# Third and fourth tile of an expert as one pair of 256 tokens, and PSUM banks of their own for first layers inside branches

## The chip, the cores and the metric

The kernel runs on one core of one Trainium2 chip. The metric is the device time of one execution in microseconds, the median of the runs shown. The engines are TensorE (PE: matmuls, PEld: weight loads), VectorE (DVE), ScalarE (ACT), GpSimd (POOL) and SyncE (SP, transfers only).

## The reference

Three parts in a row: attention with 32 global and 512 local positions, a dense block of width 2048 with a squared relu, and a block of eight experts. The change lies in the last. Cut to what matters:

```
do_compute = x @ w_skip > 0            # x: 2176 tokens of 512
logits = x[do_compute] @ w_gate        # eight experts
e_idx, gate_w = argmax and its softmax weight
for e in range(8):                     # w1[e]: 512 x 1024, w2[e]: 1024 x 512
    h = maximum(x[mask_e] @ w1[e], 0)
    y[mask_e] = gate_w * (h @ w2[e])
out[do_compute] = x[do_compute] + y
```

How many tokens an expert has is known only when the kernel runs.

## The kernel before

Tokens are first sorted into slots of 128 for each expert. An expert's tokens are worked in tiles of 128. A **tile** (`expert_tile`) is a generator in nine steps: `first` makes the hidden layer of 1024 as two blocks of 512 columns, each 4 x 3 matmuls with 128 tokens as the stationary operand and a block of 512 weight columns streaming past. Every product is done in three matmuls, high x high, high x low and low x high, as each operand is kept as a rounded high part and a remainder (names ending in `h` and `l`, or the two halves of `xp`). `turn` transposes the relu's result (four transposes, `ertr`), because the second layer needs it with the hidden index on the partitions, and splits it on ScalarE and VectorE (`split`). `second` is 24 matmuls of 512 columns into `y`. A VectorE step (`eo`) scales by the gate weight and adds the token itself, and GpSimd scatters the rows to `out`.

Before a tile runs, GpSimd **gathers** its tokens from DRAM (`gather`, into `xg`), and `prepare` transposes them (four transposes, `etr`) and splits them into `xp`. Tile 0 of every expert always runs; while it runs, the weights of the next expert are fetched, rounded on ScalarE (`e42h` is the high part of fetch 42; eight fetches an expert, so e24 to e31 are expert 3's and e32 to e39 expert 4's), and the low parts are made on VectorE (`e42l`). Each later tile stands inside the arm of a branch on the expert's number of tokens (`more`, `tc.If`): the arm of tile j starts the gather of tile j + 1, runs tile j with the preparation of tile j + 1 after its sixth step, and ends with the branch for tile j + 1. After the fifth tile there is a loop. `hint` tells the engines ahead of time which way the next branch will go. The order of instructions is the order of the code; nothing is rescheduled. Each engine passes the branch by itself, and waits behind it are on counts that each engine's semaphore has reached, the arm's share included.

The hidden layer's results lie in two PSUM banks with the tag `h`, in tile 0 and in every arm alike. `s` and `o` are the tags of two banks that attention and routing use before the experts begin, and `x2` has two banks for `y`.

The dense block (`ffn_block`) already does its first layer the other way round: weights stationary, 256 tokens moving, so that the hidden index comes out on the partitions and nothing is transposed.

## Time and profile before

| | us |
|---|---|
| median of three runs | 740.95 (740.13 to 741.21) |
| the profiled execution | 740.43 |
| its span, first to last instruction | 738.6 |
| PE busy in it | 708.3 |
| DVE, ACT, POOL busy in it | 420.2, 393.3, 168.5 |
| expert 1, first matmul of tile 0 | 595.12 |
| expert 3: tile 0, 1, 2, 3, first matmul each | 622.14, 635.26, 647.58, 660.02 |
| expert 4, 5, 6, 7, first matmul of tile 0 | 673.06, 686.51, 700.07, 713.64 |

A profile's times belong to one execution. Busy is the time in which an engine had an instruction in work; PE's ends are modelled, so two PE rows overlap on paper, and the step from start to start is the real pace. PE fetches its own code: the queue called q8 instruction carries pieces of 16 KB.

### The profile page before, as it was taken

What the parts mean: (1) busy time and instruction counts of PE and PEld (TensorE: products, weight loads), DVE (VectorE), ACT (ScalarE), POOL (GpSimd) and SP (SyncE); (2) the same over time, 40 slices, a digit from 0 to 9 for tenths busy, and PEclk for the clock granted to TensorE, in tenths of its full rate; (3) what the DMA queues carried; (4) which work ended last, traced back from release to release, by engine and by line L of the source; (5) the groups of instructions that cost most, each with busy time, mean ns of one, the idle gap of its engine ahead of it and who ended that gap; (6) DMA issues with size and microseconds to landing.
All of it is one profiled execution on the core that took longest, in us unless ns stands there. A gap on an engine that the chain in (4) does not pass through costs nothing. (4 is left out here: it accounts for less than half of the span.)

```text
span 738.6 us, 18687 instructions
## 1 busy us (share of the span) xinstructions
PE 708.3 (96%) x7509; PEld 588.1 (80%) x7509; DVE 420.2 (57%) x1077; ACT 393.3 (53%) x968; POOL 168.5 (23%) x213
## 2 busy tenths in 40 slices
PE   6689999999999999999999999999999999999996
PEld 4466677889888888888888988888878777887774
DVE  1889955853652463556165265342576279615993
ACT  5767567665544553534555454343354368515781
POOL 5000144461121121212112111122132222222121
PEclk8799999999999999999999999999999999999999
DMA  9999461073146114063501204100475779615920
GB/s 269 249 296 302 173 152 36 19 182 47 35 107 145 48 37 105 2 133 77 123 31 37 70 14 143 59 28 3 163 210 171 270 239 339 241 46 180 337 71 17
DMA packets 119462, 96.07 MB, mean 130 GB/s; under 512 B 84997, under 2 KB 92165, under 8 KB 119348
## 3 DMA queue, kind: packets, MB, share of 16 engines
q1 hardware_dynamic: 108304, 71.01, 35.0%
q10 hardware_dynamic: 8292, 15.48, 6.4%
q0 software_dynamic: 2752, 8.07, 3.4%
q8 instruction: 71, 1.16, 0.7%
q14 instruction: 43, 0.35, 0.2%
HBM read 82.28 MB, written 13.18 MB: 129 GB/s over the span
## 5 line engine op out<-in xcount | busy, mean ns | idle before, releaser
L180 POOL TENSOR_TENSOR gl<-g,gh 128x256 fp32r<-128x256 f32 x107 | 79.7, 745 | 302.2 <-ACT gh L179 154.7
L696 PE MATMUL h<-xh,w_in 128*128 128x256 f32 x464 | 134.7, 290 | 0.7 <-ACT xh L179 0.7
L697 PE MATMUL h<-xl,w_in 128*128 128x256 f32 x464 | 129.5, 279 | 0.3 <-DVE xl L180 0.3
L698 PE MATMUL h<-xh,w_in 128*128 128x256 f32 x464 | 129.7, 279 | 0.0
L721 PE MATMUL acc<-w_out,gh 128*128 128x512 f32 x232 | 97.7, 421 | 1.5 <-ACT gh L179 1.5
L723 PE MATMUL acc<-w_out,gl 128*128 128x512 f32 x232 | 91.9, 396 | 0.2
L722 PE MATMUL acc<-w_out,gh 128*128 128x512 f32 x232 | 91.6, 395 | 0.0
L696 PEld LDWEIGHTS h<-xh,w_in 128*128 128x128 f32 x464 | 87.0, 188 | 4.2 <-ACT xh L179 0.9
L700 ACT ACTIVATE g<-h 128x256 f32<-128x256 f32 x128 | 48.8, 382 | 76.7 <-PE h L698 43.3
L697 PEld LDWEIGHTS h<-xl,w_in 128*128 128x128 f32 x464 | 87.3, 188 | 2.7 <-DVE xl L180 0.5
L698 PEld LDWEIGHTS h<-xh,w_in 128*128 128x128 f32 x464 | 87.0, 188 | 0.0
L429 ACT ACTIVATE sm<-sm,mx 128x128 f32<-128x128 f32 x120 | 46.7, 391 | 49.5 <-DVE mx L427 49.5
L737 DVE TENSOR_TENSOR g<-h,g 128x256 f32<-128x256 f32 x53 | 22.2, 420 | 85.4 <-ACT g L700 85.3
L179 ACT CAST gh<-g 128x256 fp32r<-128x256 f32 x116 | 47.2, 407 | 42.2 <-DVE g L737 40.2
L723 PEld LDWEIGHTS acc<-w_out,gl 128*128 128x128 f32 x232 | 43.6, 188 | 12.0 <-POOL gl L180 1.4
L721 PEld LDWEIGHTS acc<-w_out,gh 128*128 128x128 f32 x232 | 43.6, 188 | 8.5 <-ACT gh L179 1.9
L722 PEld LDWEIGHTS acc<-w_out,gh 128*128 128x128 f32 x232 | 43.8, 189 | 5.6
L180 DVE TENSOR_TENSOR ehl<-ertr,ehl 128x512 fp32r<-128x512 f32 x26 | 18.0, 691 | 38.8 <-ACT ehl L179 38.8
L863 POOL DMA_INDIRECT xg<-x2d,slots x19 | 23.6, 1243 | 47.6 <-DVE ehl L180 15.0
L422 DVE TENSOR_TENSOR sm<-sc,mask 128x512 f32<-128x512 f32 x30 | 20.6, 687 | 23.8 <-PE sc L409 23.1
L894 ACT ACTIVATE er<-eh 128x512 f32<-128x512 f32 x26 | 15.6, 600 | 34.6 <-PE eh L891 31.1
L251 POOL TENSOR_TENSOR w_in<-st_raw_in,w_in 128x512 fp32r<-128x512 f32 x10 | 13.0, 1307 | 81.2 <-ACT w_in L247 81.2
(724 smaller groups left out, 1584.0 us busy)
## 6 DMA issues: line engine op xcount, KB each, us to landing
st_e<-in_moe_w_dram SPq DMA_DIRECT2D x52, 512.0 KB, 6.0
vr<-in_v_l_dram SPq DMA_DIRECT2D x49, 192.0 KB, 4.0
st_raw_in<-in_moe_w_in_dram SPq DMA_DIRECT2D x16, 512.0 KB, 7.4
st_raw_out<-in_moe_w_out_dram SPq DMA_DIRECT2D x16, 512.0 KB, 5.6
st_e<-in_moe_w_dram ACTq DMA_DIRECT2D x12, 512.0 KB, 4.8
x2d<-x ACTq DMA_DIRECT2D x19, 256.5 KB, 4.4
st_gv<-in_v_l_dram SPq DMA_DIRECT2D x8, 512.0 KB, 4.1
out_dram<-x ACTq DMA_DIRECT2D x16, 256.0 KB, 4.1
```

Of the source, the lines that this page charges most:

```text
L179: nc.scalar.copy(hi, src)
L180: (lo_engine or nc.vector).tensor_tensor(out=lo, in0=src, in1=hi.bitcast(F32), op=ALU.subtract)
L429: nc.scalar.activation(sm[:, hh, :], sm[:, hh, :], AF.Exp, bias=mx[:, hh:hh + 1], scale=SCALE, accum_out=osum[:, 2 * hh + g:2 * hh + g + 1],)
L696: nc.tensor.matmul(h, lhsT=wh, rhs=xh[:, k, :], start=(k == 0), stop=False)
L697: nc.tensor.matmul(h, lhsT=wh, rhs=xl[:, k, :], start=False, stop=False)
L698: nc.tensor.matmul(h, lhsT=wl, rhs=xh[:, k, :], start=False, stop=(k == KD - 1))
L700: nc.scalar.activation(g, h, AF.Relu)
L721: nc.tensor.matmul(acc[z], lhsT=gh[:, c], rhs=wh, start=first_one, stop=False)
L722: nc.tensor.matmul(acc[z], lhsT=gh[:, c], rhs=wl, start=False, stop=False)
L723: nc.tensor.matmul(acc[z], lhsT=gl[:, c], rhs=wh, start=False, stop=last_one)
L737: nc.vector.tensor_tensor(out=square, in0=h, in1=g, op=ALU.mult)
L863: nc.gpsimd.indirect_dma_start(out=gathered(e, j), out_offset=None, in_=x2d, in_offset=bass.IndirectOffsetOnAxis(ap=gi, axis=0), bounds_ch ...
```

## The change

For every expert but the first, the third and fourth tile are done together when the expert has over 384 tokens; with 257 to 384 tokens the third tile is done alone, in the other arm of that branch. The arm of tile 1 now gathers and prepares both. `expert_pair` does the first layer as the dense block does, with the two tiles' 256 tokens moving, one unit of 128 hidden positions after the other, and the second layer of a unit after the first layer of the next. The hidden units go to two banks in turn, `s` and `o`, each with its relu on ScalarE and its low part on VectorE. The fifth tile is gathered and prepared inside its own arm. The branch behind the pair gets no hint. And `inner` gives every first layer inside an arm the banks `s` and `o`, so that `h` is tile 0's alone (of expert 0, tile 0's and tile 1's, which both stand outside of branches).

```diff
     def gathered(e, j):
-        return xgs[(0, e % 3) if j == 0 else (1, e % 2) if j % 2 else (2, 0)]
+        if j == 3 and e:
+            return xgs[0, e % 3]
+        return xgs[(0, e % 3) if j == 0 else (1, e % 2) if j % 2 or (j == 4 and e) else (2, 0)]
...
     def prepared(e, j):
-        return xps[(0, e % 2) if j == 0 else (1, 0) if j == 1 else (2, j % 2)]
+        if j > 1:
+            return [x[:, :, j % 2 * P:(j % 2 + 1) * P] for x in joint()]
+        x = xps[(0, e % 2) if j == 0 else (1, 0)]
+        return x[:, 0], x[:, 1]
...
+    def inner(in_arm, z, name):
+        tag = ("s", "o")[z % 2] if in_arm else "h"
+        return ps.tile([P, 512], F32, tag=tag, bufs=BANKS[tag], name=name)
...
-                hs[fb] = ps.tile([P, 512], F32, tag="h", bufs=2, name=f"eh_{name}_{fb}")
+                hs[fb] = inner(j > (not e), fb, f"eh_{name}_{fb}")
...
+    def expert_pair(e, sis):
+
+        ph, pl = joint()
+        ys, gs = [], {}
+
+        def first(f):
+            fb, c = divmod(f * P, DM)
+            cols = slice(c, c + P)
+            h = inner(True, f, f"eph_{e}_{f}")[:, 0:BLK]
+            for k in range(KD):
+                wh, wl = ew[e, 1, (fb, k)]
+                nc.tensor.matmul(h, lhsT=wh[:, cols], rhs=ph[:, k, :], start=(k == 0), stop=False)
+                nc.tensor.matmul(h, lhsT=wh[:, cols], rhs=pl[:, k, :], start=False, stop=False)
+                nc.tensor.matmul(h, lhsT=wl[:, cols], rhs=ph[:, k, :], start=False, stop=(k == KD - 1))
+            gh, gl = gs[f] = [sb(n, 3, [P, BLK], f"e{n}_{e}_{f}", F32R) for n in ("gh", "gl")]
+            nc.scalar.activation(gh, h, AF.Relu)
+            nc.vector.scalar_tensor_tensor(
+                out=gl, in0=h, scalar=0.0, in1=gh.bitcast(F32), op0=ALU.max, op1=ALU.subtract
+            )
+
+        def second(f):
+            gh, gl = gs.pop(f)
+            wh, wl = ew[e, 2, f]
...
+            for z in range(2):
+                c = slice(z * P, (z + 1) * P)
+                nc.tensor.matmul(ys[z], lhsT=gh[:, c], rhs=wh, start=(f == 0), stop=False)
+                nc.tensor.matmul(ys[z], lhsT=gh[:, c], rhs=wl, start=False, stop=False)
+                nc.tensor.matmul(ys[z], lhsT=gl[:, c], rhs=wh, start=False, stop=(f == KE - 1))
+
+        first(0)
+        for f in range(KE):
+            if f + 1 < KE:
+                first(f + 1)
+            second(f)
...
         def least(e, j):
+            if e and j == 2:
+                return 3 * P
...
-                if j + 1 < UNROLL:
-                    hint(e, j + 1)
-                    gather(e, j + 1, slot(gidx, e, j + 1))
+                if e and j == 4:
+                    gather(e, j, slot(gidx, e, j))
+                    prepare(e, j)
+                    following = ()
+                else:
+                    following = (2, 3) if e else range(j + 1, UNROLL)[:1]
+                    if following:
+                        hint(e, j + 1)
+                for z in following:
+                    gather(e, z, slot(gidx, e, z))
                 for u, _ in enumerate(expert_tile(e, j, slot(sidx, e, j))):
-                    if u == 5 and j + 1 < UNROLL:
-                        prepare(e, j + 1)
-                more(e, j + 1)
+                    if 5 <= u < 5 + len(following):
+                        prepare(e, following[u - 5])
+                more(e, j + 1) if j != 1 else more_two(e)
...
+        def more_two(e):
+
+            with tc.If(n_tok[e] > least(e, 2), label=f"more{e}_2") as branch:
+                expert_pair(e, [slot(sidx, e, z) for z in (2, 3)])
+                more(e, 4)
+            with branch.Else():
+                with tc.If(n_tok[e] > 2 * P):
+                    for _ in expert_tile(e, 2, slot(sidx, e, 2)):
+                        pass
```

On PE, the start of expert 3's third tile. Ahead of it stand the last matmuls of tile 1 (`y_3_1`) and the branch. Before, a tile follows:

```order
L905 MATMUL y_3_1_10354<-e31l_10283,ehl_3_1_10353 128x512
L906 MATMUL y_3_1_10354<-e31h_10259,ehl_3_1_10353 128x512
L1166 COMPARE_AND_BRANCH
L1151 REGISTER_ALU
L1225 BRANCH_PREFETCH_HINT
L889 MATMUL eh_3_2_0_10456<-e24h_9623,xp2_0_8023 128x512 [waits Activation_49]
L890 MATMUL eh_3_2_0_10456<-e24l_9644,xp2_0_8023 128x512
L891 MATMUL eh_3_2_0_10456<-e24h_9623,xp2_0_8023 128x512 [waits DVE_49]
```

Now the pair follows (`eph_3_0` is its first unit):

```order
L916 MATMUL y_3_1_10539<-e31l_10465,ehl_3_1_10538 128x512
L917 MATMUL y_3_1_10539<-e31h_10441,ehl_3_1_10538 128x512
L1249 COMPARE_AND_BRANCH
L958 MATMUL eph_3_0_10628<-xp2_0_8023,e24h_9714 128x256 [waits Activation_49]
L959 MATMUL eph_3_0_10628<-xp2_1_8024,e24h_9714 128x256 [waits DVE_49]
L960 MATMUL eph_3_0_10628<-xp2_0_8023,e24l_9735 128x256
```

Tokens and weights have changed places, the columns are 256, the hint is gone, and the wait for VectorE's low part of the tokens moved from the third matmul to the second.

Further on in the same place on PE, where the hidden layer goes over into the second layer. Before, in tile 2 (`ertr` are the transposes of the hidden layer):

```order
L891 MATMUL eh_3_2_1_10471<-e27h_10202,xp2_0_8023 128x512
L904 MATMUL y_3_2_10455<-e28h_10208,ehl_3_2_10454 128x512 [waits Activation_49]
L905 MATMUL y_3_2_10455<-e28l_10224,ehl_3_2_10454 128x512
L906 MATMUL y_3_2_10455<-e28h_10208,ehl_3_2_10454 128x512 [waits DVE_49]
L904 MATMUL y_3_2_10455<-e28h_10208,ehl_3_2_10454 128x512
L905 MATMUL y_3_2_10455<-e28l_10224,ehl_3_2_10454 128x512
L906 MATMUL y_3_2_10455<-e28h_10208,ehl_3_2_10454 128x512
L276 MATMUL ertr_3_2_1_10499<-ident_70,er_3_2_1_10491 128x128 [waits Activation_49]
```

Now, in the pair (`yp_3_0` and `yp_3_1` are the outputs of the two halves, `egh` and `egl` the parts of a hidden unit):

```order
L960 MATMUL eph_3_1_10645<-xp2_0_8023,e25l_9754 128x256
L974 MATMUL yp_3_0_10662<-e28h_10390,egh_3_0_10641 128x512 [waits Activation_49]
L975 MATMUL yp_3_0_10662<-e28l_10406,egh_3_0_10641 128x512
L976 MATMUL yp_3_0_10662<-e28h_10390,egl_3_0_10642 128x512 [waits DVE_49]
L974 MATMUL yp_3_1_10663<-e28h_10390,egh_3_0_10641 128x512
L975 MATMUL yp_3_1_10663<-e28l_10406,egh_3_0_10641 128x512
L976 MATMUL yp_3_1_10663<-e28h_10390,egl_3_0_10642 128x512
L958 MATMUL eph_3_2_10670<-xp2_0_8023,e24h_9714 128x256
```

The transposes are gone, and the second layer of a unit waits for ScalarE once and for VectorE once, with the next unit's first layer ahead of it.

On PE, the end of expert 3's arms, ahead of expert 4's first tile (`eh_4_0_0`). Before, the ends of four arms:

```order
L1166 UNCONDITIONAL_BRANCH [waits PE_49] x4
L889 MATMUL eh_4_0_0_10836<-e32h_10281,xp0_0_8020 128x512 [waits Activation_49]
L890 MATMUL eh_4_0_0_10836<-e32l_10302,xp0_0_8020 128x512 [waits DVE_49]
L891 MATMUL eh_4_0_0_10836<-e32h_10281,xp0_0_8020 128x512 [waits DVE_49]
L889 MATMUL eh_4_0_0_10836<-e32h_10281,xp0_0_8020 128x512
```

Now the other arm's tile 2 (`y_3_2`) stands there, and three ends behind it:

```order
L917 MATMUL y_3_2_11033<-e31h_10441,ehl_3_2_11032 128x512
L1253 UNCONDITIONAL_BRANCH
L1253 UNCONDITIONAL_BRANCH [waits PE_49]
L1227 UNCONDITIONAL_BRANCH [waits PE_49]
L900 MATMUL eh_4_0_0_11109<-e32h_10463,xp0_0_8020 128x512 [waits Activation_49]
L901 MATMUL eh_4_0_0_11109<-e32l_10484,xp0_0_8020 128x512 [waits DVE_49]
```

From the branch behind the pair to expert 4's first matmul lie the arm of the fifth tile, the loop and now the other arm as well.

## Rows read from the trace of the kernel before

**Rows 1.** The page's first table: busy us (share of the span) x instructions.

```profile
PE 708.3 (96%) x7509; PEld 588.1 (80%) x7509; DVE 420.2 (57%) x1077; ACT 393.3 (53%) x968; POOL 168.5 (23%) x213
```

**Rows 2.** Busy us by stage: tile 2, tile 3, expert 5 (columns in the first line).

```profile
core 0: us, PE busy (x) PEld busy (x) DVE busy (x) ACT busy (x) POOL busy (x), PEclk, DMA share, GB/s
...
647.58:660.02 12.44, 12.44 (x62) 10.19 (x61) 2.83 (x4) 2.96 (x5) 2.06 (x2) 1.00 0.13 42
660.02:673.06 13.04, 12.60 (x61) 10.01 (x60) 3.23 (x5) 4.32 (x7) 2.05 (x2) 1.00 0.14 43
...
686.51:700.07 13.56, 13.29 (x64) 10.43 (x65) 12.58 (x14) 11.11 (x14) 3.07 (x3) 1.00 0.97 337
```

**Rows 3.** Timeline (start, us, engine, line, what, [idle before]): two ends of tiles.

```profile
647.36 0.39 PE L906 MATMUL y<-e31h,ehl 128*128 128x512 f32 x1
...
647.58 0.40 PE L889 MATMUL eh<-e24h,xp 128*128 128x512 f32 x1
...
672.23 0.39 PE L906 MATMUL y<-e31h,ehl 128*128 128x512 f32 x1
...
673.06 0.50 PE L889 MATMUL eh<-e32h,xp 128*128 128x512 f32 x1 [0.44 <-PEq L1166]
```

**Rows 4.** Instructions of tile eh in expert 3: xcount, duration ns min/median/max, first and last start.

```profile
L889 PE MATMUL eh<-e24h,xp x8: 389/393/498, 622.1 to 660.7; 128*128 128x512 f32 x8
```

**Rows 5.** Timeline of PE: one group of transposes inside the second layer.

```profile
644.39 0.60 PE L276 MATMUL etr<-ident,xg 128*128 128x128 f32 x4
...
644.75 0.48 PE L904 MATMUL y<-e30h,ehl 128*128 128x512 f32 x1
...
645.06 0.39 PE L905 MATMUL y<-e30l,ehl 128*128 128x512 f32 x1
```

**Rows 6.** Timeline of PE in the dense block; group of its weight loads (busy, mean ns).

```profile
519.93 0.28 PE L696 MATMUL h<-xh,w_in 128*128 128x256 f32 x1
...
521.35 0.40 PE L721 MATMUL acc<-w_out,gh 128*128 128x512 f32 x1
...
522.75 0.39 PE L721 MATMUL acc<-w_out,gh 128*128 128x512 f32 x1
...
L697 PEld LDWEIGHTS h<-xl,w_in 128*128 128x128 f32 x464 | 87.3, 188 | 2.7 <-DVE xl L180 0.5
```

**Rows 7.** Timeline there: a unit's last matmul, its relu, VectorE's step.

```profile
521.23 0.28 PE L698 MATMUL h<-xh,w_in 128*128 128x256 f32 x1
...
521.61 0.39 ACT L700 ACTIVATE g<-h 128x256 f32<-128x256 f32 x1 [1.18 <-PE h L698]
...
522.03 0.42 DVE L737 TENSOR_TENSOR g<-h,g 128x256 f32<-128x256 f32 x1 [1.07 <-ACT g L700]
```

**Rows 8.** Timeline: a prepared tile's low part, and the start of expert 3's tile 1.

```profile
634.69 0.69 DVE L180 TENSOR_TENSOR xp<-etr,xp 128x512 fp32r<-128x512 f32 x1
...
635.03 0.39 PE L906 MATMUL y<-e31h,ehl 128*128 128x512 f32 x1
...
635.26 0.39 PE L889 MATMUL eh<-e24h,xp 128*128 128x512 f32 x1
```

**Rows 9.** The gather in tile 1: timeline, and DMA issues (us to landing).

```profile
638.79 1.02 POOL L863 DMA_INDIRECT xg<-x2d,slots  x1 [0.31 <-issue]
...
xg<-x2d,slots POOLq DMA_INDIRECT x1, 3.5
```

**Rows 10.** Timeline: from expert 4 to expert 5.

```profile
685.84 0.40 PE L906 MATMUL y<-e39h,ehl 128*128 128x512 f32 x1
...
686.51 0.50 PE L889 MATMUL eh<-e40h,xp 128*128 128x512 f32 x1 [0.27 <-ACTq L1166]
...
688.38 1.23 DVE L834 TENSOR_TENSOR e42l<-st_e,e42h 128x1024 fp32r<-128x1024 f32 x1 [0.40 <-DVEq L1166]
...
689.66 0.19 PEld L890 LDWEIGHTS eh<-e42l,xp 128*128 128x128 f32 x1 [0.30 <-DVE e42l L834]
```

**Rows 11.** Fetches of PE's code (packets, MB, share): whole span, and from 670 to 671.

```profile
q8 instruction: 71, 1.16, 0.7%
...
q8 instruction: 1, 0.02, 5.5%
```

## The prediction

> **What bounds the kernel now.** I read the page's busy table first: TensorE is busy 96% of the span [rows 1]. Then the table by stages, cut at the starts of the tiles of expert 3 and after [rows 2]: in the two tiles that the change fuses, VectorE and ScalarE have 2.8 to 4.3 us of work in 12 to 13 us, TensorE has 12.4 to 12.6 at a granted clock of 1.00. There, and only there, TensorE alone sets the pace. In the experts that follow, VectorE is busy 12.58 of 13.56 us, so those stages have two limits. Last the timeline of TensorE: tile 2 begins 0.22 us after the last matmul of tile 1 was issued, which is the ordinary step, so a branch that is taken costs nothing; from the last matmul of tile 3 to the first of expert 4 it is 0.83 us, so the branch that is not taken, with the ends of the arms behind it, costs 0.60 [rows 3]. Whatever is saved on TensorE between 647.58 and 673.06 should arrive at the end in full: the transfers are quiet there (share 0.13 to 0.14), expert 4's first weights are converted, and everything later hangs on the end of the arms.

> **Is the new arm entered at all?** Expert 3's first weight block is multiplied eight times with one line, two for each tile, so four tiles ran and the expert has over 384 tokens [rows 4]. No other expert has a third and a fourth tile, so one pair is made in the whole run.

> **What goes.** Each tile has 24 + 24 matmuls of 512 columns and groups of four transposes between them. A group takes a slot of 0.36 us from its start to the next matmul, and that matmul's successor comes 0.31 us later where 0.23 is usual [rows 5]: 0.44 us a group. Tiles 2 and 3 have two groups each for the hidden layer (0.44 x 4 = 1.76 us), and tile 3 has one more for a fifth tile that never runs (0.44). These go. The group that prepares tile 3 doesn't go, it moves from tile 2 into tile 1. What is left of a tile is (12.44 - 3 x 0.44) / 48 = 0.232 us for a matmul.

> **What comes.** The first layer of the pair is turned round: weights stationary, 256 token columns moving, 8 x 12 matmuls of 256 columns. The dense block before it in the kernel does the same, so its timeline gives the price: 12 such matmuls from 519.93 to 521.35, 0.118 each, then 6 of 512 columns to 522.75, 0.233 each, 2.82 us together [rows 6]. The pair is eight such units: 8 x 2.82 = 22.56 us.

> **Does the new pipeline hold?** A unit's result must pass ScalarE (relu) and VectorE (the low part) before the second layer uses it, one unit of lag later. In the dense block the relu starts 0.38 us after the last matmul's issue and VectorE's step of the same 256 columns ends 0.42 after 522.03 [rows 7]: 0.77 us for the high part, 1.22 for the low. The pair's first use of the high part comes 0.12 + 1.42 = 1.54 us after that issue, of the low part 0.47 later at 2.01. About 0.75 us is left on both, so I cost this at nothing. For the last unit the cover is the 1.40 us of the second layer before it, which is as long. If the cover were gone, each of eight units would pay the shortfall.

> **The start of the pair.** The prepared tile 3 is now used at once. At the start of tile 1, whose preparation lies at the same place, the low part ends at 634.69 + 0.69 = 635.38, with the last matmul issued at 635.03 and the first of the new tile at 635.26 [rows 8]. A tile first reads the low part in its third matmul, 0.46 after the first, the pair in its second, about 0.12 after the first: 635.38. That is even, so 0.07 us (between 0 and 0.23). Two gathers instead of one go to GpSimd's queue at the start of tile 1; a gather is issued in 1.02 us and lands 3.5 us after issue [rows 9], so the second, about 1.3 us behind the one at 638.79, is there at 643.6, and its transposes come near 646. Nothing. The second scatter of the pair (1.02 us on GpSimd) and VectorE's second output step lie behind the last matmul, where expert 4's tile has its weights already; I cost them at nothing, and at 0.1 if VectorE's first low part for expert 4 is late by that.

> **The end of the pair.** Before, 0.60 us. After, there is one arm fewer to close but a jump over the other arm; I keep 0.60, with 0 (a branch as free as the taken one) and 0.85 (one more closing step of 0.25) as ends.

> **The banks.** Before, the first matmul of each expert is held by ScalarE's branch: 0.67 us after the last issue at 685.84, 0.44 more than a step [rows 10], because the arms may have used the same banks. With own banks that wait should go, at five transitions outside the arms. But a little later the same matmul stream stands still for the low part of a weight (0.30 us on the weight loader at 689.66, released by VectorE's e42l, which ran from 688.38) [rows 10]. VectorE reaches that part through its own queue, without TensorE's gap in the way: low parts, splits, the output step, its own branch (0.40). So a TensorE that starts 0.3 to 0.4 earlier waits that much longer at e42l and its kin. I cost the banks at nothing.

> **The sum.** From 647.58 to 673.06 it is 25.48 us. After: 0.44 (the preparation moved into tile 1) + 0.07 + 22.56 + 0.60 = 23.67. The difference is -1.81 us. By parts: -1.76 - 0.44 for the groups, +0.24 for 96 matmuls at 0.118 against 48 at 0.232, +0.08 for the other 48, +0.07: the same. The profiled execution takes 740.43 us (span 738.6) and should become 738.6; the median of the three runs is 740.95, which gives 739.1. Ends of this case: if the second layer runs at the 0.227 of the fastest tiles (0.32 less), a group costs 0.36 instead of 0.44 and the end of the pair costs nothing, 738.1; if start and end cost their most, 739.55.

> **Rivals.** *The banks pay too.* If VectorE's chain is not the limit at the five transitions, 0.27 to 0.44 us is won at each, some 1.7 us: 737.4. For it: TensorE does wait there. Against: the wait at e42l comes behind it each time.

> *Code arrives late.* The branch behind the pair has no hint (before, the branch behind tile 3 had one), it is not taken, and a second jump leads over the other arm. Counting a matmul as its load and its multiply, the first jump passes some 250 instructions, the second 115. One fetch of code is 16 KB and keeps one DMA engine for 0.007 x 16 x 738.6 / 71 = 1.17 us [rows 11]. If one stands in the open: 740.3. Against it: TensorE's queue runs ahead, since a fetch stands between 670 and 671 [rows 11], over one us before the last matmul of tile 3 is issued, and the matmuls around it keep their step. [...]

> *Slower: weight loads set the pace of the narrow matmuls.* Each of the 96 needs its own load of 188 ns [rows 6] and streams for 118. In tiles of 512 columns a load always fits beside a matmul. Were the loads not overlapped, the pair would pay 96 x 0.07 = 6.7 us: 745.8. It passes the 0.2% on the slow side once some 47 loads stand in the open (3.3 us). Against it: the dense block has the same loads and still steps at 0.118. [...] The rows here say 0.118 against 0.233, almost exactly half, and I go by them.

> *Nothing changes* (the arm isn't entered): 740.95; excluded by the four tiles but for the count lying at a border.

> **How the numbers follow.** Forecast 0.68, banks 0.10, late code 0.16, slower 0.04, nothing 0.02. A measurement here can tell about 0.2%, 1.48 us, so faster means under 739.47. The forecast's 0.68 lies below that with 0.57 and within it with 0.11; with the banks' case faster has 0.67, same 0.27 (0.11 + 0.14 + 0.02), slower 0.06 (0.04 and 0.02 of the late code, with several fetches). The range reaches from the banks' 737.4 to one open fetch with a little on top, 740.4.

> **What would show it.** After: from the first matmul of the pair to the first of expert 4 some 23.2 us; 96 matmuls stepping at 0.118 and no idle before the second layer's; tile 1 at 12.8 us; the gap at the end of the pair near 0.8. First matmuls of experts without a wait for ScalarE's branch, and a longer wait for e18l, e26l, e42l, e50l, e58l. I am wrong if the pair's units take over 2.9 us, if the gap behind the pair is over 1.5 us (code), or if the periods of the last experts fall below 13.4 us (banks).

## The result, and the profile after

The changed kernel takes 745.77 us (median of 10 runs, 741.74 to 747.82) against 740.99 (739.4 to 742.0, also 10 runs) for the kernel before: a ratio of 1.0065, 95% interval 1.0047 to 1.0082. It is slower by more than the 0.2% (1.48 us) that the prediction counts as telling, where 739.1 and "faster" were forecast. Its runs also scatter over 6 us, those of the kernel before over 2.6. The profiled execution took 747.72 us with a span of 746.0 (before: 740.43 and 738.6).

TensorE's busy time grew by 3 us, although there are fewer columns to stream (five groups of transposes less). The page's busy table of the kernel after, to be held against [rows 1]:

```profile
PE 711.3 (95%) x7537; PEld 591.4 (79%) x7537; DVE 420.4 (56%) x1080; ACT 391.1 (52%) x967; POOL 167.6 (22%) x212
```

The table by stages shows where. Its rows are expert 4, expert 5 and expert 6 of the kernel after, each from its first matmul to that of the next expert, and two short stretches inside the first and the third of them:

```profile
core 0: us, PE busy (x) PEld busy (x) DVE busy (x) ACT busy (x) POOL busy (x), PEclk, DMA share, GB/s
...
672.81:687.68 14.87, 14.73 (x64) 11.66 (x65) 10.59 (x12) 9.09 (x12) 4.74 (x3) 0.89 0.89 303
687.68:701.26 13.58, 13.40 (x64) 10.43 (x65) 12.58 (x14) 11.11 (x15) 2.87 (x2) 1.00 0.93 316
701.26:721.25 19.99, 15.00 (x65) 11.68 (x65) 13.65 (x15) 12.00 (x16) 3.68 (x4) 0.91 0.28 90
...
672.81:677.72 4.91, 4.91 (x14) 3.87 (x15) 3.10 (x3) 0.54 (x2) 0.00 (x0) 0.65 0.96 332
...
708.32:712.30 3.98, 3.98 (x12) 3.24 (x13) 2.22 (x2) 0.59 (x2) 1.14 (x1) 0.57 0.22 59
```

Before, experts 4, 5 and 6 took 13.45, 13.56 and 13.57 us. Expert 5 is as it was; expert 4 is 1.4 us longer at a granted clock of 0.65 over its first 5 us, and expert 6 is 6.4 us longer: it stands still for 5 us (3.79 inside it and 1.20 at its end), and 4 us more run at a clock of 0.57. Expert 3, where the change is, takes 50.67 us from its first matmul (622.14) to expert 4's (672.81), against 50.92. Together that is 7.6 us, the difference of the two spans (7.4) but for 0.2.

TensorE's timeline of the kernel after (start, us, engine, line, what, [idle before]) at the four places that matter: the start of the pair, its end, expert 6 and the start of expert 7:

```profile
648.19 0.28 PE L958 MATMUL eph<-xp,e24h 128*128 128x256 f32 x1
648.36 0.38 PE L959 MATMUL eph<-xp,e24h 128*128 128x256 f32 x1
648.58 0.28 PE L960 MATMUL eph<-xp,e24l 128*128 128x256 f32 x1
...
670.62 0.40 PE L976 MATMUL yp<-e31h,egl 128*128 128x512 f32 x1
672.81 0.50 PE L900 MATMUL eh<-e32h,xp 128*128 128x512 f32 x1 [1.79 <-ACT e36h L828]
...
704.14 0.39 PE L900 MATMUL eh<-e50h,xp 128*128 128x512 f32 x1
708.32 0.74 PE L901 MATMUL eh<-e50l,xp 128*128 128x512 f32 x1 [3.79 <-DVE e50l L834]
708.86 0.63 PE L902 MATMUL eh<-e50h,xp 128*128 128x512 f32 x1
...
719.65 0.40 PE L917 MATMUL y<-e55h,ehl 128*128 128x512 f32 x1
721.25 0.47 PE L900 MATMUL eh<-e56h,xp 128*128 128x512 f32 x1 [1.20 <-PEq L1227]
```

The pair itself does what was forecast. Its last matmul starts at 670.62, where tile 3's last started at 672.23 [rows 3]. Then the gain is lost three times:

- **Behind the pair** the step to expert 4 is 2.18 us, before 0.83 [rows 3].
- **In expert 6** TensorE waits 3.79 us for the low part of weight 50.
- **Behind expert 6** the step to expert 7 is 1.59 us, before 0.67.

The releaser that a row names has to be looked at. The first gap is put down to ScalarE's conversion of weight 36, and ScalarE's timeline has it ending at 672.20, 0.6 us before TensorE starts. The second gap ends with VectorE, and VectorE itself is late. The timelines of ScalarE and of VectorE:

```profile
671.15 1.05 ACT L828 CAST e36h<-st_e 128x1024 fp32r<-128x1024 f32 x1 [0.99 <-PEq L1227]
```

```profile
702.12 0.74 DVE L938 SCALAR_TENSOR_TENSOR eo<-y,xg 128x512 f32<-128x512 f32 x1
707.04 1.23 DVE L834 TENSOR_TENSOR e50l<-st_e,e50h 128x1024 fp32r<-128x1024 f32 x1 [4.18 <-DVEq L1227]
```

Before, the same two steps of VectorE (line 927 is its output step there) lay 0.40 us apart:

```profile
700.80 0.74 DVE L927 SCALAR_TENSOR_TENSOR eo<-y,xg 128x512 f32<-128x512 f32 x1
701.95 1.23 DVE L834 TENSOR_TENSOR e50l<-st_e,e50h 128x1024 fp32r<-128x1024 f32 x1 [0.40 <-DVEq L1166]
```

"DVEq" and "PEq" are the engines' own sequencers, and line 1227 is the branch. The trace also keeps every branch instruction with its duration, though it isn't counted as busy. TensorE's branches over an expert's arms, which nobody enters in experts 1, 2, 4, 5 and 6, took 0.35 to 0.39 us before at every one of the five. After, the one behind expert 6 took 3.46 us, and the jump over the other arm behind the pair 1.54 us, from 671.21 to 672.75. VectorE's first instruction of any kind behind its branch of expert 5 came 3.81 us after the output step had ended; behind experts 1, 2, 4 and 6, and before at all five, that is 0.04 us. A packet of TensorE's code, 16 KB, was moved from 670.16 to 671.23, and another from 718.58 to 719.54. The table of DMA queues of the kernel after has the first of them, from 670 to 671 us:

```profile
q8 instruction: 1, 0.02, 6.7%
```

Both branches ended some 1.5 us after their packet. That is so throughout: in the fourteen profiles of this document 23 of TensorE's branches behind 600 us took over 0.6 us, and each ended 1.36 to 1.59 us after a packet of its code had landed. VectorE's stalls (five in all) each ended 1.47 to 1.62 us after a packet of the queue q14, which carries the code of the other engines in pieces of 8 KB. (In the kernel before, from 20 to 554 us, 51 packets of q8 go with 12908 recorded instructions of TensorE, 253 to a packet, and 20 of q14 with 2491 of the other four engines, 125 to a packet.) So the three stalls look like waits for code.

### The profile page after: what moved, and what is told of

It is laid out like the page before. It is cut to its first block, busy times and chain, and to the rows that moved or that the text cites. A ratio compares the mean times of both kernels' runs of the same rounds, so it can differ in the third digit from the quotient of the medians.

```text
span 746.0 us, 18723 instructions
## 1 busy us (share of the span) xinstructions
PE 711.3 (95%) x7537; PEld 591.4 (79%) x7537; DVE 420.4 (56%) x1080; ACT 391.1 (52%) x967; POOL 167.6 (22%) x212
## 5 line engine op out<-in xcount | busy, mean ns | idle before, releaser
L180 DVE TENSOR_TENSOR ehl<-ertr,ehl 128x512 fp32r<-128x512 f32 x22 | 15.2, 691 | 30.0 <-ACT ehl L179 30.0
L739 ACT ACTIVATE g<-g 128x256 f32<-128x256 f32 x63 | 26.2, 416 | 5.5 <-ACT g L700 2.8
```

The source lines that it names most:

```text
L180: (lo_engine or nc.vector).tensor_tensor(out=lo, in0=src, in1=hi.bitcast(F32), op=ALU.subtract)
L739: nc.scalar.activation(square, g, AF.Square)
```

## The experiments

Three theories. **Code:** the branches wait for instructions, since the change moves where the code lies. TensorE's code of an expert with all its arms grew by 172 instructions, VectorE's by 3 (counted in the programs); most of it never runs. **Scatter:** GpSimd issues the pair's second scatter only when the first has landed, and everything behind it is late. **Banks:** the new banks make the engines meet at other moments. The scatter theory has its rows, GpSimd's timeline of the kernel after:

```profile
671.39 1.01 POOL L990 DMA_INDIRECT out_dram<-eop,slots  x1 [20.53 <-DVE eop L986]
679.68 0.99 POOL L990 DMA_INDIRECT out_dram<-eop,slots  x1 [7.28 <-DMA out_dram<-eop,slots]
681.78 2.06 POOL L871 DMA_INDIRECT xg<-x2d,slots  x1 [1.11 <-DVE e37l L834]
```

All results together. Times are medians; each ratio is to the runs of the kernel before beside it (medians 740.2 to 741.0). The kernel one_scatter leaves out a write (below). The last three columns are from the one profile of each kernel: TensorE's last branch behind the pair (before: behind tile 3), its branch behind expert 6, and VectorE's delay behind its branch of expert 5, in us.

| kernel | us | ratio (95%) | pair | exp. 6 | VectorE |
|---|---|---|---|---|---|
| before | 740.99 | | 0.19 | 0.36 | 0.04 |
| after | 745.77 | 1.0065 (1.0047 to 1.0082) | 1.54 | 3.46 | 3.81 |
| again | 747.09 | 1.0081 (1.0055 to 1.0108) | 1.50 | 3.49 | 3.22 |
| pad_pe | 745.51 | 1.0052 (1.0034 to 1.0070) | 0.19 | 0.36 | 3.47 |
| pad_dve | 740.86 | 1.0006 (0.9992 to 1.0020) | 1.74 | 3.73 | 0.04 |
| pad_both | 739.51 | 0.9981 (0.9969 to 0.9994) | 0.19 | 0.36 | 0.04 |
| pad_dve8 | 742.86 | 1.0036 (1.0023 to 1.0049) | 1.34 | 2.77 | 0.04 |
| one_scatter | 742.35 | 1.0022 (1.0009 to 1.0034) | 1.84 | 3.53 | 0.04 |
| pair_only | 759.19 | 1.0237 (1.0206 to 1.0267) | 1.72 | 2.90 | 3.15 |
| banks_only | 740.56 | 0.9999 (0.9985 to 1.0012) | 0.19 | 0.35 | 0.04 |
| no_else | 738.35 | 0.9965 (0.9949 to 0.9982) | 0.18 | 0.35 | 0.04 |
| no_else_5 | 738.69 | 0.9971 (0.9957 to 0.9985) | 0.18 | 0.36 | 0.04 |
| pad_before | 750.70 | 1.0131 (1.0092 to 1.0170) | 0.20 | 3.50 | 0.04 |
| small | 750.44 | 1.0128 (1.0112 to 1.0143) | 0.18 | 0.35 | 0.04 |

### The same kernel again

> The changed kernel once more, nothing edited, for a second profile of it. Theories. CODE: the time comes from three stalls at branches (TensorE's jump over the other arm behind the pair, 1.54 us in the first profile; VectorE's branch behind expert 5, 3.81 us; TensorE's branch behind expert 6, 3.46 us) and from the slower clock behind two of them. SCATTER: it comes from GpSimd, whose second scatter of the pair waited 7.3 us for the first. BANKS: it comes from the new PSUM banks, which put the engines in another phase. CODE expects a median of 744 to 747 with a spread of 4 us or more, the stall behind the pair (TensorE's step from pair to expert 4 over 2 us) and the one behind expert 6 (branch over 2 us) at the same places, as the code lies where it lay; VectorE's may come or not, since its fetch runs beside weight traffic. SCATTER expects the 7 us wait on GpSimd again and TensorE waiting for a prepared tile. BANKS says nothing of the places.

747.09 us, 745.61 to 748.67 over five runs, so 3 us of spread and not 4. All three stalls are at the same places with nearly the same lengths, VectorE's too (a fourth, 1.24 us behind expert 4, is new). These three belong to the program, not to chance. The fourth branch took 0.45 us in the first profile of the same program, so not every length does.

### One half of the change at a time

The pair without its banks:

```diff
-        tag = ("s", "o")[z % 2] if in_arm else "h"
+        tag = "h"
```

> The changed kernel with the first layers of the arms back in the banks that they had before; only the pair is left of the change. CODE expects the time of the changed kernel, 743 to 747, with the step of over 2 us behind the pair: the code is as long as before this edit. SCATTER expects the same, since both scatters are still there, but with the loss behind GpSimd. BANKS expects the forecast of the pair alone, 739 to 740.

All three expected less: 759.19 us. The waits of TensorE from 597 to 728 us (what waited, for whom; total, times, longest), TensorE's timeline from expert 1 to 2 and VectorE's beside it:

```profile
PE eh L900 <- DVEq L1227: 10.9, 4, 5.1
PE eh L900 <- ACT e36h L828: 2.2, 1, 2.2
```

```profile
607.96 0.40 PE L917 MATMUL y<-e15h,ehl 128*128 128x512 f32 x1
610.31 0.47 PE L900 MATMUL eh<-e16h,xp 128*128 128x512 f32 x1 [1.95 <-DVEq L1227]
```

```profile
609.36 0.74 DVE L938 SCALAR_TENSOR_TENSOR eo<-y,xg 128x512 f32<-128x512 f32 x1
610.50 1.23 DVE L834 TENSOR_TENSOR e18l<-st_e,e18h 128x1024 fp32r<-128x1024 f32 x1 [0.40 <-DVEq L1227]
```

In the arms of before only ScalarE read the first layer's banks, so the next expert's first matmul waited for ScalarE's branch, 0.27 us [rows 10]. In the pair VectorE reads them too, for the low part of the hidden layer. An arm that *may* have run then makes TensorE wait for VectorE's branch as well, which lies behind the output step of the tile just done: 2.35 us from expert to expert instead of 0.67 behind experts 1, 2, 4 and 6 (5.46 behind expert 5, where VectorE itself stalls as well), though only expert 3 makes a pair. So the banks are what the pair needs. Alone they bring nothing:

```diff
-                hs[fb] = ps.tile([P, 512], F32, tag="h", bufs=2, name=f"eh_{name}_{fb}")
+                hs[fb] = inner(j > (not e), fb, f"eh_{name}_{fb}")
...
-        h = ps.tile([P, 512], F32, tag="h", bufs=2, name="eh_rest")[:, 0:fw]
+        h = inner(True, 0, "eh_rest")[:, 0:fw]
```

> The kernel before with only the banks of the change: first layers in the arms use the other two banks. TensorE's step between experts should fall from 0.67 to 0.55 at five places, as in the changed kernel, so 0.6 us less if nothing behind takes it back: 740.1 to 740.7. If the banks are what the time comes from, 744 or more. The code is as long as before, so CODE expects no stall.

740.56 us, a ratio of 0.9999. The step between experts fell from 0.67 to 0.55 at the five places and nothing came of it.

### Code that never runs

The loop for a sixth tile of an expert runs for nobody here. Matmuls or memsets put into it are never executed; they shift the code behind them. With the memsets VectorE and SyncE execute what they did before. The matmuls also change a little that is executed: two waits more on SyncE among the weights' transfers (before 612 us) and one condition less in a wait of VectorE at 686 us.

```diff
                     for _ in expert_tile(e, UNROLL, si):
                         pass
+                    if e == 3:
+                        pad = sb("xt", 1, [P, 3 * BLK], "pad")[:, 0:P]
+                        for _ in range(88):
+                            nc.vector.memset(pad, 0.0)
+                    if e == 0:
+                        pad = ps.tile([P, DM], F32, tag="x2", bufs=2, name="pad")
+                        for _ in range(64):
+                            nc.tensor.matmul(pad, lhsT=prepared(e, UNROLL)[0][:, 0, :], rhs=ew[e, 2, 0][0], start=True, stop=True)
```

The first four added lines alone are pad_dve (with 8 for 88 pad_dve8), the last four alone pad_pe, all of them pad_both.

> The changed kernel with 64 matmuls more in the loop for a sixth tile of expert 0, which never runs here: nothing executed differs, only TensorE's code from expert 1 on lies 128 instructions further. CODE expects the stalls of TensorE to move: the one behind expert 6 (3.46 us) gone, others behind experts 1, 4 and 5, where now a block of 256 ends between the hint and the branch; the time 744 to 752. If where the code lies doesn't matter (SCATTER, BANKS), the time is the changed kernel's within 0.3%, and the places are the same.

TensorE's stall behind expert 6 is gone, and the one behind the pair too, which had not been foretold. Of the three new ones expected, one came (1.93 us behind expert 1); behind experts 4 and 5 the branches took 0.49 and 0.36. The one that came didn't show in the steps (0.55), since some 2 us of matmuls were queued ahead of it (in the kernel after that branch starts at 605.91, and expert 1's last matmul at 608.03). VectorE's stall stayed, as its code had not moved, and with it most of the time.

> The changed kernel with two pieces of code that never run: 64 matmuls more in expert 0's loop for a sixth tile (as in the run before) and 88 memsets of VectorE in expert 3's loop. What is executed is the changed kernel, instruction for instruction; the code of TensorE lies 128 instructions further from expert 1 on, VectorE's 88 further from expert 4 on. CODE expects VectorE's stall behind expert 5 (3.2 to 3.8 us in four profiles so far, always there) to be gone, as its branch and its target then lie in one block of 128; TensorE's step behind the pair 0.83 as in the run with TensorE's code shifted alone; no slow clock: 738.5 to 740.5, that is 5 to 7 us less than the changed kernel for code that is never run. If where the code lies doesn't matter for VectorE, 745 to 746 with the stall at its place.

739.51 us: 0.2% under the kernel before, and 6 to 8 us under the changed kernel, whose instructions are executed here but for the waits named above. VectorE's and TensorE's timelines at the two places of the stalls:

```profile
702.50 1.23 DVE L834 TENSOR_TENSOR e50l<-st_e,e50h 128x1024 fp32r<-128x1024 f32 x1 [0.40 <-DVEq L1235]
```

```profile
672.78 0.40 PE L976 MATMUL yp<-e31h,egl 128*128 128x512 f32 x1
673.61 0.50 PE L900 MATMUL eh<-e32h,xp 128*128 128x512 f32 x1 [0.43 <-PEq L1235]
```

The step behind the pair is 0.83, as before the change. GpSimd's second scatter is still late, 7.0 us behind the first (8.3 in the kernel after), its timeline says:

```profile
673.54 1.01 POOL L990 DMA_INDIRECT out_dram<-eop,slots  x1 [20.53 <-DVE eop L986]
680.55 1.35 POOL L990 DMA_INDIRECT out_dram<-eop,slots  x1 [6.00 <-DVE ehl L180]
```

So the scatter theory falls: with that wait in place the loss is gone. In no_else below it is 8.6 us, and the loss is gone too.

> The changed kernel with the 88 never-run memsets of VectorE alone, to complete the square of none, TensorE, VectorE and both. CODE expects VectorE's stall behind expert 5 gone and TensorE's two left (1.5 us behind the pair, 3.5 us at the branch behind expert 6): 741.5 to 743.5, between both (739.5) and none (745 to 747). If VectorE's stall hangs on GpSimd's late second scatter and not on where VectorE's code lies, it stays, and the time is 745 to 747.

740.86 us, a little less than expected, VectorE's stall gone, TensorE's two at their places. That fills the square: 747.09 with neither piece of code (745.77 in the first ten runs), 745.51 with TensorE's, 740.86 with VectorE's, 739.51 with both. VectorE's place is worth some 5 to 6 us. TensorE's is worth 1.4 with VectorE's stall gone, and 0.3 or 1.6 beside it, by which of the two medians one takes.

The same test on the kernel before, 55 matmuls in the loop of expert 0:

> The kernel before with 55 matmuls more in expert 0's loop for a sixth tile, which never runs: nothing executed differs, TensorE's code from expert 1 on lies 110 instructions further, so that in each expert a block of 256 ends 31 to 49 instructions behind the hint (it was 31 and 52 in the two places that stalled). CODE expects branches of 1.5 to 3.5 us on TensorE behind several of the experts 1, 2, 4, 5, 6 instead of 0.36; up to some 1.9 us of each lies behind matmuls that are already queued, so 741 to 747. If only the change itself brings the stalls, 740.8 and 0.36 at each.

750.70 us (747.33 to 755.14 over four runs, over the 741 to 747 expected): about 10 us for code that is never run, with nothing of the change in it. The two waits on SyncE and the one condition on VectorE are the same as in pad_pe and pad_both, where stalls went; so those don't decide. TensorE's branches behind experts 1, 2, 4, 5 and 6 took 3.31, 4.56, 5.34, 4.42 and 3.50 us, all five that were named, and up to 5.34 where at most 3.5 was expected. The waits of TensorE from 597 to 728 us have them, and its timeline the worst:

```profile
PE eh L889 <- PEq L1170: 8.1, 6, 3.0
```

```profile
690.29 0.40 PE L906 MATMUL y<-e39h,ehl 128*128 128x512 f32 x1
693.67 0.77 PE L889 MATMUL eh<-e40h,xp 128*128 128x512 f32 x1 [2.99 <-PEq L1170]
```

### Without the second scatter

```diff
-        for z in range(2):
+        for z in range(1):
             nc.gpsimd.indirect_dma_start(
                 out=out, out_offset=bass.IndirectOffsetOnAxis(ap=sis[z], axis=0), in_=os[z], in_offset=None,
```

> The changed kernel without the second scatter of the pair: the rows of expert 3's fourth tile are not written. GpSimd then has no wait of 7 us between two scatters, and the gathers behind it are issued earlier. SCATTER expects most of the loss back: under 742. CODE expects nothing from it: 745 to 748, with the stalls of TensorE behind the pair and behind expert 6 and of VectorE behind expert 5 at their places.

The rows of expert 3's fourth tile are not written here. A miss of the code theory: 742.35 us, and VectorE's stall behind expert 5 is gone. GpSimd is early, as its timeline shows, and so is VectorE at expert 6:

```profile
673.25 1.01 POOL L990 DMA_INDIRECT out_dram<-eop,slots  x1 [20.52 <-DVE eop L986]
675.24 1.18 POOL L871 DMA_INDIRECT xg<-x2d,slots  x1 [0.98 <-issue]
```

```profile
705.42 1.23 DVE L834 TENSOR_TENSOR e50l<-st_e,e50h 128x1024 fp32r<-128x1024 f32 x1 [0.40 <-DVEq L1227]
```

What differs is a fetch. From 688 to 701 us, around expert 5, the table of DMA queues of the kernel after has code for TensorE alone (q8); with one scatter it has packets of the queue that serves the other engines (q14) as well, the second of them 0.8 us behind VectorE's output step of expert 4, from where VectorE enters expert 5:

```profile
q1 hardware_dynamic: 2044, 3.95, 89.0%
q0 software_dynamic: 96, 0.20, 4.1%
q8 instruction: 2, 0.03, 1.3%
```

```profile
q8 instruction: 2, 0.03, 1.0%
q14 instruction: 2, 0.02, 0.4%
```

All profiles divide in this way. In the four with the stall behind expert 5 (after, again, pad_pe, pair_only) no packet of q14 starts for 12 us behind that step; in the other ten one starts 0.07 to 3.9 us behind it. The queue serves several engines, so whose code it was is not shown.

VectorE's code lay where it had lain in the kernel after but for one instruction, so either that instruction or GpSimd's earlier work decided. A small shift with both scatters was to tell:

> The changed kernel with 8 never-run memsets in the place of the 88. In the run without the second scatter VectorE's stall behind expert 5 went away, though VectorE's code lay where it had lain but for one instruction. If the place of the code alone decides, and coarsely (branch and target of expert 5 in two blocks of 128, as before this shift), the stall stays here: 745 to 747; then the run without the second scatter lost it through GpSimd, and both are needed. If it goes away here too (742 to 743), single instructions of shift decide, and that run says nothing of GpSimd.

742.86 us, and the stall behind expert 5 is gone; a smaller one, 1.34 us, stands behind expert 6. So a shift of a few instructions is enough, and the run without the second scatter says nothing about GpSimd. That the kernels with both scatters and none of the stalls (pad_both, no_else) are faster than before speaks against GpSimd too.

### Less code

The other arm taken out, so that 257 to 384 tokens take the pair too:

```diff
         def least(e, j):
-            if e and j == 2:
-                return 3 * P
             return j * P + (SEG if (e, j) == (E - 1, 1) else 0)
...
-            with branch.Else():
-                with tc.If(n_tok[e] > 2 * P):
-                    for _ in expert_tile(e, 2, slot(sidx, e, 2)):
-                        pass
```

> The changed kernel without the other arm: an expert with 257 to 384 tokens takes the pair too, so there is no second jump behind the pair, and each expert's arms are 115 TensorE instructions shorter. CODE expects the step from pair to expert 4 back at 0.7 to 0.9 us instead of 2.18, and no slow clock behind it: 2.9 us less there. The stall behind expert 6 should be gone or elsewhere, since all later code lies otherwise (counted in the program, the blocks of 256 instructions end between hint and branch in experts 2 and 7, so those two may stall): 739 to 744. SCATTER expects 745 to 746, since both scatters are there. BANKS expects no difference, 745 to 746.

> The kernel without the other arm once more, in more rounds, as the version that may beat both: an expert with 257 to 384 tokens takes the pair. CODE expects no stall on VectorE behind expert 5 and none behind the pair: 737.5 to 739.5, which is 1 to 2 us under the kernel before, the forecast of the pair with its banks.

738.35 and 738.69 us, ratios of 0.9965 and 0.9971: faster than both kernels. All the branches named in the table are short again, no matmul of 512 columns in experts 1 to 7 is at the slow clock, and the only wait of TensorE from 597 to 728 us is the step behind the pair, with its timeline:

```profile
PE eh L900 <- PEq L1225: 0.4, 1, 0.4
```

```profile
670.95 0.40 PE L976 MATMUL yp<-e31h,egl 128*128 128x512 f32 x1
671.78 0.51 PE L900 MATMUL eh<-e32h,xp 128*128 128x512 f32 x1 [0.43 <-PEq L1225]
```

The guess in its expectation that experts 2 and 7 might stall was wrong for expert 2 (0.35 us) and nearly so for 7 (0.66). What of this gain is the missing arm and what the new place of the code is not told apart: pad_both keeps the arm and has 739.51.

Then the arm for a fifth tile was taken out as well, so that the loop stands directly behind the pair:

```diff
-                with tc.For_i(UNROLL, (n_tok[e] + (P - 1)) // P, 1) as it:
+                with tc.For_i(4 if e else UNROLL, (n_tok[e] + (P - 1)) // P, 1) as it:
...
-                more(e, 4)
+                more(e, UNROLL)
```

> The same with the arm for a fifth tile taken out as well (the loop, which never runs here, would do fifth tiles): TensorE's code is 124 instructions shorter in each expert. CODE expects nothing from less code as such, only from where it comes to lie: 737.5 to 740 if no branch stalls. If the length of the jumps decides, it is faster than the version above by 0.3 us or more at each expert: under 737.

A bad version, for a reason of its own: 750.44 us. TensorE's timeline behind the pair:

```profile
672.78 0.40 PE L976 MATMUL yp<-e31h,egl 128*128 128x512 f32 x1
681.84 0.79 PE L900 MATMUL eh<-e32h,xp 128*128 128x512 f32 x1 [8.66 <-issue]
```

The loop makes no round, but it is no longer inside an arm that is skipped. In the trace all five engines come together behind it and go through one list of semaphores, transfers' among them, of which the first is fulfilled at 680.23, 2.6 us after the second scatter's issue: 9.06 us from the pair to expert 4 instead of 0.83. It says nothing on the length of jumps.

## Why the prediction was wrong, point by point

- **What bounds the kernel, and the pair's price: right.** In no_else, from the pair's first matmul (648.52) to expert 4's (671.78) it is 23.26 us; 23.2 were forecast. Tile 1 takes 12.79 (12.8). Expert 3 takes 49.31 us instead of 50.92, so 1.61 are saved where 1.81 were worked out. Of the rest, 0.15 stands in tile 0 (13.27 instead of 13.12 us), where the start that the banks bring forward is given back. In the kernel after, twelve matmuls of the first unit take 1.57 us, 0.15 more than the block's 1.42: the start of the pair, costed at 0.07 between 0 and 0.23.
- **Slower by weight loads: fell.** The matmuls of 256 columns step at 0.12 us.
- **The banks at nothing: right for the banks alone** (0.9999), with 0.12 us a step where 0.27 to 0.44 had been allowed. The text missed what they are for. It never asked who reads the first layer's banks in the new arm; with the pair and without the banks the kernel takes 759.19 us.
- **The second scatter at nothing: right,** although its wait of 7 to 8.6 us was not foreseen.
- **The end of the pair: wrong.** 0.60 was kept with 0.85 as its upper end; it is 1.95 (a step of 2.18 less 0.23). The rival of late code had the place, the unhinted second jump. The argument against it was that TensorE's queue runs ahead: a fetch stood between 670 and 671 [rows 11], in time for a matmul at 673.06. Here a fetch also stands between 670 and 671, but the jump comes at 671.21, just as that packet ends (671.23); that it waited for this very packet is read from the times, not shown. Its price was too low: 1.17 us, the packet's own time. The branch ended 1.5 us after the packet had landed, and behind the wait the clock fell for eight matmuls, at 0.42 us a step instead of 0.23, another 1.5 us. That the place of the code did it, and not the jump as such, pad_pe and pad_both show: the second jump is in both, and the step is 0.83.
- **The step that failed most is one that isn't in the sum.** Every term of it costs instructions that are executed. What never runs was costed at nothing without a sentence on it. 172 TensorE instructions more in each expert, and 3 of VectorE's, moved all the code behind them against the blocks in which it is fetched, and that brought the stalls behind experts 5 and 6, 6.4 us of the 7.6 in the profile, three experts after the place that the prediction looked at. The list of what would prove it wrong did name a gap of over 1.5 us behind the pair as code; it had nothing for a stall elsewhere.

That a branch waits for a fetch is the author's reading of the times: the long branches, up to 5.34 us on TensorE (pad_before), each ended 1.36 to 1.59 us after a packet. The traces also show hinted branches over all the arms of an expert in 0.35 to 0.39 us (before), so the wait doesn't always come; whether it is the hint that hides the fetch, and what makes that fail, no run here shows.

What stays open is the rule: which places make a fetch late was not found, for neither engine. The expectations name experts by counting where blocks of code end, of 256 instructions for TensorE and 128 for VectorE, an estimate that goes with the 253 and 125 recorded to a packet. That named all five stalls of pad_before, but of the five named for pad_pe and no_else only one came in full (1.93 us), so it isn't a rule. Nor does the place alone set the length: TensorE's code lies the same in after, again, pad_dve, pad_dve8 and one_scatter, and its branch behind expert 4 took 0.45, 1.24, 0.78, 1.22 and 0.46 us. That the place of the code is the cause was shown in both directions: the changed kernel lost its stalls by code that is never run, and the kernel before gained five.

## What to carry to other kernels

Code that never runs was not free here, some 10 us in pad_before. In a kernel with branches look at the branch instructions of the trace, all engines, everywhere behind a change that lengthens an arm, and try the kernel with some dead instructions before its time is believed; a result of 1% either way may be the place of the code. Of two ways to write a rare case try the one with less code: without the other arm the kernel took 738.4 to 738.7 instead of 745.8, though 739.5 came with the arm in place and the code shifted, so most of it may be the place again. And ask of each buffer in an arm which engines read it, since here the code behind a skipped arm waited for all of them (pair_only: 2.35 us from expert to expert instead of 0.67).
